# An attention, soft mixture and feed-forward kernel whose attention order is searched at build time and whose copies may change engine

## Chip, cores and metric

The kernel runs on one core of one Trainium2 chip. The metric is the device time of one execution in microseconds (us); for the kernel before, three executions gave 387.11 us as median, from 385.46 to 387.39 us.

## What is computed

Three parts follow each other, cut here to what matters:

```python
# 1 attention, B=4, H=8, S=576, D=64
mask_plain = (rel >= 0) & (rel < 32)                          # heads 0-3
mask_dil = (rel >= 0) & (rel < 128) & (rel % 4 == 0)          # heads 4-7
scores = where(mask, q @ k.T / 8, -1e9)
attn = exp(scores - scores.max(-1)); attn /= attn.sum(-1) + 1e-9
x = (attn @ v).transpose(0, 2, 1, 3).reshape(2304, 512)
# 2 soft mixture of experts, 8 experts with 4 slots each
logits = x @ phi                                              # 2304 x 32
d = softmax(logits, over tokens);  slot_input = d.T @ x
slot_out[e] = relu(slot_input[e] @ w1[e]) @ w2[e]             # w1: 512x1024, w2: 1024x512
y = softmax(logits, over slots) @ slot_out
# 3 feed-forward, d_ff = 2048
h = y @ w_in;  out = (max(h, 0) + alpha * min(h, 0)) @ w_out
```

## The kernel before

The kernel has three stages in one program. **Attention** works on 16 units (a batch and two heads) of nine blocks of 64 queries; eight blocks form a group, so there are 18 groups `g`. A group goes through a fixed chain of steps:

- `sm` and `s` (PE, L273 and L282): the mask is put into a PSUM bank, then 32 matmuls add the scores.
- `max` and `sub` (DVE, L293, L296), `exp` (ACT, L299), `sum` and `rec` (DVE, L303, L307, L308), `norm` (POOL, L312).
- `t` (PE, L317): four transposes; `te` (ACT, through `copy`, L346): two copies of 64x512 from PSUM into `pt_m`.
- `pv` (PE, L330): 32 matmuls; `ev`: their eviction into `xt`, one half on ACT (L346), the other on DVE (L348).

Around these stand the steps of a unit. `qx` (`emit_qx`, L252) spreads a unit's loaded queries into two padded copies, one half of the partitions on ACT (L346) and the other on DVE (L348). When a unit is complete, `lt` (L360) adds its part of the logits; for every second unit `x` and `xe` (L401, L404) transpose tokens and copy them into `xs_m`, on ACT, DVE, ACT in turn; once a batch, `nmax`, `dexp`, `lts`, `lrun`, `dT`, `dTe`, `part` and `acc` (L363 to L421) carry the running softmax over tokens.

All loads are issued by SP, in one order: `q` and `k` of a pair of units (L250, 576 KB each; the first pair in 288 KB pieces), `v` of a unit (L259, 576 KB), and expert weights `w` (L187, 1 MB each; 12 have a buffer of their own, `w0` to `w11`). A `q` load waits until the `qx` copies have emptied the buffer, a `v` load until the `pv` of four units before has read it. A load that waits holds up every load behind it on SP.

The order of the whole stage is written by `schedule` (L82). `tasks_of_attention` (L428) lists tasks with their engine, what they need, a key (a due time, `PERIOD` 4.3 us a group) and two costs from the table `COST`: how long the engine is occupied and after how long the result is there. `schedule` holds a clock for each engine (and one for the DMAs), takes again and again the task that could start first, the smaller key among equals, emits it, and moves that engine's clock on. It adds a margin where a result crosses engines: 0.6 us if PE is the one that waits, 0.25 us for the others here. So it is a plan made at build time; on the chip each engine keeps the planned order and waits on semaphores. The planned order is the only thing that the chip sees of it.

After `schedule` (L548) a hand-written tail (L557 to L600) finishes the last batch. Then the **mixture** stage reads 32 weights of 1 MB (`emit_l1` L622, `emit_l2` L637 to L653), its order written by hand, and the **feed-forward** stage starts with `conv(0, 0)` (L701, ACT), which needs the first feed-forward weight (L185, `w_f`, the 33rd 1 MB load) and stands behind the copy L753 on ACT. The feed-forward stage is planned by the same `schedule`, with costs, places and keys of its own (L937).

## Time and profile before

| | us |
|---|---|
| median of three executions | 387.11 (385.46 to 387.39) |
| the profiled execution | 387.63 |
| its span, first to last instruction | 385.9 |
| PE busy | 366.5 (95%) |
| DVE busy | 261.9 (68%) |
| ACT busy | 217.2 (56%) |
| POOL busy | 144.0 (37%) |
| DMA | 75.19 MB, mean 195 GB/s |

The profiled execution took 1.7 us more than its span, the time outside the first and last instruction. A share of busy time is an average over three stages with different limits: attention with its tail fills the span to about 99 us, the mixture to about 140 us, the feed-forward the rest. The DMA engines work until about 150 us nearly without a break and little after that. Matmuls are pipelined and the profile models their ends, so a PE that is shown as busy may still run at half its clock; the granted clock is shown beside it.

### The profile page before, as it was taken

The page shows a single profiled execution, that of the slowest core. Times are in us where ns is not written, and L with a number is a line of the kernel's source. Part 1 is how long each engine was busy: PE and PEld are TensorE (multiplying, and loading weights), DVE is VectorE, ACT ScalarE, POOL GpSimd, SP SyncE. Part 2 cuts the span into 40 slices and gives each one's busy share as a digit, 9 for nine tenths or more (in the row PEclk, how much of TensorE's full clock was granted, in tenths as well). Part 3 has the DMA queues.
Part 4 walks back from the last instruction along what each step waited for, and adds up shares of the span by engine and source line. Part 5 has one row for each costly group of instructions (what it writes and reads, how often), then busy time and mean ns, then how long its engine had stood idle before and what let it go on. Part 6 is the DMA issues. An engine that isn't in the chain of part 4 may idle for free.

```text
span 385.9 us, 7887 instructions
## 1 busy us (share of the span) xinstructions
PE 366.5 (95%) x3126; PEld 273.7 (71%) x3126; DVE 261.9 (68%) x452; ACT 217.2 (56%) x467; POOL 144.0 (37%) x125
## 2 busy tenths in 40 slices
PE   8599998998999988899999999999999999999995
PEld 4488786765444357577877787877788878878884
DVE  5968977874237439999999998939974324234263
ACT  2657777675123228888766846646654545446460
POOL 4322222230000004555455566445564444444460
PEclk9979999999899998999999999999999999999999
DMA  8989999999999996053233225000000000001336
GB/s 297 415 324 395 413 414 359 404 416 419 420 419 422 417 422 245 10 207 118 102 112 124 104 100 204 15 0 0 3 1 0 2 0 0 3 0 62 103 122 205
DMA packets 15156, 75.19 MB, mean 195 GB/s; under 512 B 1904, under 2 KB 2304, under 8 KB 8976
## 3 DMA queue, kind: packets, MB, share of 16 engines
q1 hardware_dynamic: 14144, 72.98, 48.5%
q10 hardware_dynamic: 912, 1.64, 1.2%
q8 instruction: 24, 0.39, 0.4%
q14 instruction: 12, 0.10, 0.1%
q0 software_dynamic: 64, 0.07, 0.1%
HBM read 69.97 MB, written 4.72 MB: 194 GB/s over the span
## 4 chain that ended last, share of the span: by engine, by line
PE 57%; DVE 24%; DMA 7%; ACT 5%; issue 4%; POOL 1%; SPq 0%; DVEq 0%; ACTq 0%; POOLq 0%
PE y L835 31%; DMA q_m<-qk 6%; DVE gs L829 5%; PE h L629 4%; PE o L651 4%; PE pv L330 3%; PE hb L821 2%; DVE wo_lo L718 2%; PE s L282 2%; DVE e_m L705 2%; DVE pt_m L711 2%; DVE e_m L708 2%; PE si L410 2%; PE x L401 2%; DVE e_m L703 1%
## 5 line engine op out<-in xcount | busy, mean ns | idle before, releaser
L929 POOL TENSOR_TENSOR gls<-gs,ghs 128x384 fp32r<-128x384 f32 x96 | 118.6, 1252 | 166.6 <-ACT ghs L346 138.3
L835 PE MATMUL y<-wo_hi,ghs 128*128 128x512 f32 x289 | 96.6, 398 | 1.0 <-ACT ghs L346 0.7
L829 DVE SCALAR_TENSOR_TENSOR gs<-gs,beta_s,hb 128x384 f32<-128x384 f32 x96 | 56.4, 609 | 50.5 <-ACT gs L923 48.5
L835 PE MATMUL y<-wo_lo,ghs 128*128 128x512 f32 x289 | 88.7, 392 | 0.0
L835 PE MATMUL y<-wo_hi,gls 128*128 128x512 f32 x289 | 85.8, 393 | 2.7 <-POOL gls L929 2.6
L923 ACT ACTIVATE gs<-hb 128x384 f32<-128x384 f32 x96 | 44.7, 492 | 36.3 <-PE hb L821 28.6
L835 PEld LDWEIGHTS y<-wo_hi,gls 128*128 128x128 f32 x289 | 54.0, 188 | 15.2 <-POOL gls L929 4.8
L346 ACT CAST ghs<-gs 128x384 fp32r<-128x384 f32 x96 | 49.4, 517 | 26.6 <-DVE gs L829 26.2
L835 PEld LDWEIGHTS y<-wo_hi,ghs 128*128 128x128 f32 x289 | 53.4, 188 | 14.6 <-issue 1.8
L835 PEld LDWEIGHTS y<-wo_lo,ghs 128*128 128x128 f32 x289 | 54.0, 188 | 10.4 <-issue 0.2
L312 POOL TENSOR_TENSOR e_m<-e_m,l 128x512 f32<-128x512 f32 x18 | 19.7, 1094 | 60.9 <-DVE l L308 48.5
L821 PE MATMUL hb<-cpack,mpack 128*128 128x384 f32 x96 | 31.3, 345 | 0.2
L282 PE MATMUL s<-q_m 128*64 128x64 f32 x576 | 21.7, 232 | 1.8 <-DVE l L307 1.4
L282 PEld LDWEIGHTS s<-q_m 128*64 128x64 f32 x576 | 19.5, 145 | 4.8 <-issue 2.4
L330 PEld LDWEIGHTS pv<-pt_m,v_m 128*64 128x64 f32 x576 | 19.0, 143 | 4.8 <-ACT pt_m L346 2.6
L346 ACT COPY pt_m<-t 64x512 f32<-64x512 f32 x36 | 20.8, 578 | 2.7 <-PE t L317 2.1
L330 PE MATMUL pv<-pt_m,v_m 128*64 128x64 f32 x576 | 21.0, 229 | 0.3
L821 PEld LDWEIGHTS hb<-cpack,mpack 128*128 128x128 f32 x96 | 17.9, 188 | 4.0 <-DVE gs L829 0.9
L348 DVE COPY xt<-pv 128x256 f32<-128x256 f32 (+7 forms) x32 | 9.6, 305 | 11.8 <-ACT xt L346 11.6
L703 DVE TENSOR_SCALAR pt_m<-pt_m 128x1024 f32<-128x1024 f32 (+1 forms) x9 | 8.1, 901 | 13.9 <-ACT pt_m L701 13.9
L632 ACT ACTIVATE v_m<-h,rinv 128x256 f32<-128x256 f32 x8 | 3.8, 474 | 22.2 <-PE h L629 22.2
L346 ACT COPY xt<-pv 128x256 f32<-128x256 f32 (+7 forms) x32 | 8.7, 279 | 10.8 <-DVE xt L348 6.5
(157 smaller groups left out, 501.7 us busy)
## 6 DMA issues: line engine op xcount, KB each, us to landing
w<-w SPq DMA_DIRECT2D x23, 1024.0 KB, 11.7
v_m<-v SPq DMA_DIRECT2D x16, 576.0 KB, 7.7
q_m<-w_f SPq DMA_DIRECT2D x8, 1024.0 KB, 4.9
q_m<-qk SPq DMA_DIRECT2D x13, 576.0 KB, 6.8
v_m<-w_f SPq DMA_DIRECT2D x7, 1024.0 KB, 4.9
q_m<-w SPq DMA_DIRECT2D x4, 1024.0 KB, 16.2
v_m<-w SPq DMA_DIRECT2D x2, 1024.0 KB, 15.0
q_m<-qk SPq DMA_DIRECT2D x4, 288.0 KB, 5.4
```

Of the source, the lines that this page charges most:

```text
L282: mm(s[r:r + 64, col:col + 64], lhsT=q_of(u)[:, 2 * o:2 * o + 64], rhs=keys(u, c, x), start=False, stop=True, skip_group_check=True)
L312: nc.gpsimd.tensor_tensor(out=e, in0=e, in1=bc(e_[g, "l"], 128, 8, 64), op=ALU.mult)
L330: mm(pv[hs, n], lhsT=vv[u % 4][:, c, hs], rhs=pts[:, NBS * (g % 2) + n, h], start=True, stop=True, skip_group_check=True)
L346: nc.scalar.copy(out=out, in_=in_)
L629: mm(h[32 * g:32 * g + 32, 0:256], lhsT=slotT[:, k, :], rhs=w[:, k % 2, 256 * g:256 * g + 256], start=(k == 0), stop=(k == 3), skip_group_ ...
L651: mm(o[32 * g:32 * g + 32, :], lhsT=ht[:, 4 * r + g, 28 - 4 * e:60 - 4 * e], rhs=w[:, g, :], start=(e == 0 and r == 0), stop=(e == NE - 1 ...
L703: nc.vector.tensor_scalar(out=t, in0=t, scalar1=2.0 ** -15, scalar2=FMAX, op0=ALU.max, op1=ALU.min)
L821: mm(hb[i], lhsT=mpack[:, 128 * f:128 * f + 128], rhs=cpack[:, t0:t0 + 384], start=True, stop=True)
L829: nc.vector.scalar_tensor_tensor(out=g, in0=g, scalar=beta_s[:, f:f + 1], in1=hb[i], op0=ALU.mult, op1=ALU.add)
L835: mm(y[steps[s][0], t][:, sl], lhsT=g, rhs=wo_hl[p == 1][:, f, sl], start=start, stop=stop, skip_group_check=True)
L923: lambda s=s, i=i: nc.scalar.activation(out=half(gs, s, i, 4), in_=hb[i], func=AF.Relu, scale=-1.0),
L929: lambda s=s, i=i: nc.gpsimd.tensor_tensor(out=half(gls, s, i, 6), in0=half(gs, s, i, 4), in1=half(ghs, s, i, 6).bitcast(F32), op=ALU.subt ...
```

## The change

`schedule` is split in two. `plan` makes one order, as `schedule` did, from the keys and from a choice of engine for the tasks that may have several. `schedule` calls it once with the old keys and the first choice, and then, for attention, 2500 times more: each round adds random numbers to the keys of 1, 3 or 10% of the tasks (loads excepted) and redraws a third of that share of the engine choices. It goes on from a round whose planned end is not later than the one it came from by more than a small random allowance, and keeps the earliest planned end of all. The planned end leaves the `w` loads out. The seed is fixed. The order kept is then emitted. The feed-forward's call has no rounds, so there `plan` runs once.

```diff
+ROUNDS = 2500
+def plan(tasks, key, pick, succ, place, lag, readers, margin, begin, mode):
...
+    def spec(name):
+        t = tasks[name]
+        return t[4][pick[name]] if name in pick else (t[0], *t[4:6])
...
+            if best is None or (at, key[name]) < best[0]:
+                best = (at, key[name]), name
...
+def schedule(tasks, place=lambda name: None, lag=lambda name, x: 0.0, readers=lambda name: (), margin=0.06, begin={},
+             mode=lambda name: None, rounds=0, spread=(2, 6, 15), counts=lambda name: True):
...
+    def run(key, pick):
+        p = plan(tasks, key, pick, succ, place, lag, readers, margin, begin, mode)
+        return (max(e[0] for n, e in p[1].items() if counts(n)), p) if p else (1e9, None)
+
+    best, p = run(key, pick)
+    top = best, p, pick
+    for _ in range(rounds):
+        k, c, share, width = dict(key), dict(pick), rng.choice((0.01, 0.03, 0.1)), rng.choice(spread)
+        for n in k:
+            if tasks[n][0] != "dma" and rng.random() < share:
+                k[n] += rng.uniform(-width, width)
+            if n in c and rng.random() < share / 3:
+                c[n] = rng.randrange(len(tasks[n][4]))
+        e, q = run(k, c)
+        if e <= best + 0.25 * rng.random() ** 3:
+            best, p, key, pick = e, q, k, c
+            if e < top[0]:
+                top = e, q, c
+    p, pick = top[1:]
+    for n in p[0]:
+        tasks[n][1](*((tasks[n][4][pick[n]][0],) if n in pick else ()))
```

The tasks with a choice, and what else moves: `qx` may go to ACT, DVE or POOL (there as a product with ones), `te`, `ev` and `xe` to ACT or DVE, each with a planned cost by engine. `s` and `pv` are now chained to the group before, `dexp` to the batch before, `xe` to the `qx` of units 2 and 3, whose raw queries lie in the same buffer. The addition of 1e-9 in `rec` becomes a `tensor_tensor` with a tile that a new memset fills.

```diff
+        if eng == "pool":
+            nc.gpsimd.tensor_tensor(out=out, in0=in_, in1=ones_s[r].rearrange("p (a b) -> p a b", b=1).to_broadcast([64, S // 32, 32]),
+                                    op=ALU.mult)
...
-        nc.vector.tensor_scalar(out=l, in0=l, scalar1=1e-9, scalar2=None, op0=ALU.add)
+        nc.vector.tensor_tensor(out=l, in0=l, in1=eps_s.to_broadcast([128, 8]), op=ALU.add)
...
-        copy("act", pts[r, n:n + NBS, :, x], t_[g][r].rearrange("p (n h q) -> p n h q", h=2, q=32))
+        copy(eng, pts[r, n:n + NBS, :, x], t_[g][r].rearrange("p (n h q) -> p n h q", h=2, q=32))
...
-                        eng = ("act", "dve")[h]
-                        task(("qx", u, h), eng, lambda u=u, h=h, e=eng: emit_qx(u, h, e),
-                             [("q", u if p == 0 else 2 * p)] + ([("s", last[u - NQ])] if u >= NQ else []), k - 5.0, "qx%d" % h)
+                        either(("qx", u, h), lambda e, u=u, h=h: emit_qx(u, h, e),
+                               [("q", u if p == 0 else 2 * p)] + ([("s", last[u - NQ])] if u >= NQ else []), k - 5.0,
+                               **dict([("act", 0.67), ("dve", 0.62)][::1 - 2 * h] + [("pool", 1.15)]))
...
-                task(("te", g, x), "act", lambda g=g, x=x: emit_te(g, x), [("t", g), ("pv", g - 2)], k + 6.0)
+                either(("te", g, x), lambda e, g=g, x=x: emit_te(g, x, e), [("t", g), ("pv", g - 2)], k + 6.0, act=0.58, dve=0.67)
...
-                    task(("ev", g, u, x), eng, lambda g=g, u=u, x=x, e=eng: emit_ev(g, u, x, e), [("pv", g)] + old,
-                         k + 9.0 + x)
+                    either(("ev", g, u, x), lambda e, g=g, u=u, x=x: emit_ev(g, u, x, e), [("pv", g)] + old, k + 9.0 + x,
+                           **dict([*cols(w).items()][::1 - 2 * x]))
...
-        schedule(tasks_of_attention(), readers=readers, margin=0.25, begin=BEGIN, mode=lambda name: MODE.get(name[0]))
+        schedule(tasks_of_attention(), readers=readers, margin=0.25, begin=BEGIN, mode=lambda name: MODE.get(name[0]),
+                 rounds=ROUNDS, counts=lambda name: name[0] != "w")
```

## Rows read from the trace of the kernel before

**Rows 1.** Chain of waits that ended last, 133 to 150 us: start, length, what.

```profile
139.02 1.04 PE o L651 x8
140.08 0.04 ACT acc_m L753
140.56 0.68 ACT pt_m L701
```

**Rows 2.** L185's instructions from 120 to 121 us, with issue and time to landing.

```profile
L185 SPq DMA_DIRECT2D q_m<-w_f x1: 327/327/327, 120.1 to 120.1; - x1
DMA to landing us min/median/max: 19.8/19.8/19.8
```

**Rows 3.** Stretches of the span: length, busy time of each engine, granted clock, DMA.

```profile
24.00:27.00 3.00, 3.00 (x57) 2.31 (x53) 1.59 (x4) 1.24 (x4) 1.04 (x1) 0.94 0.54 131
27.00:60.00 33.00, 31.38 (x620) 25.02 (x619) 27.34 (x68) 25.16 (x58) 8.41 (x8) 1.00 1.02 408
60.00:64.00 4.00, 4.00 (x55) 2.26 (x53) 3.87 (x10) 3.20 (x7) 0.28 (x1) 1.00 0.79 277
64.00:83.00 19.00, 18.38 (x370) 14.78 (x370) 15.08 (x40) 13.72 (x34) 5.39 (x5) 1.00 1.01 409
83.00:140.00 57.00, 54.77 (x642) 27.39 (x636) 23.27 (x58) 16.38 (x43) 1.98 (x3) 0.97 1.01 420
```

**Rows 4.** What SP's queue waited for until 90 us: total, times, longest.

```profile
SPq L259 <- PE pv L330: 23.4, 10, 4.8
SPq L250 <- DVE q_m L348: 19.6, 6, 5.8
```

**Rows 5.** Two more stretches, as in rows 3.

```profile
8.00:18.00 10.00, 6.30 (x145) 4.87 (x139) 8.82 (x18) 4.83 (x10) 2.28 (x2) 0.98 1.02 405
18.00:24.00 6.00, 5.72 (x81) 5.01 (x83) 3.61 (x10) 3.14 (x6) 1.24 (x1) 0.50 1.02 415
```

**Rows 6.** Timeline of PE, 15 to 100 us: start, length, instruction, idle time before it.

```profile
18.28 1.12 PE L282 MATMUL s<-q_m 128*64 128x64 f32 x16 [1.44 <-DVE l L307]
...
20.81 1.98 PE L330 MATMUL pv<-pt_m,v_m 128*64 128x64 f32 x32
...
27.39 1.15 PE L330 MATMUL pv<-pt_m,v_m 128*64 128x64 f32 x32
...
59.77 0.63 PE L317 MATMUL t<-eye_s,e_m 128*128 128x128 f32 x4 [1.50 <-DVE xs_m L348]
...
91.68 0.53 PE L360 MATMUL lt<-xt,phi_s 128*32 128x192 f32 x6 [0.93 <-DVE xt L348]
```

**Rows 7.** L250's instructions from 11 to 11.2 us.

```profile
L250 SPq DMA_DIRECT2D q_m<-qk x1: 327/327/327, 11.0 to 11.0; - x1
DMA to landing us min/median/max: 7.1/7.1/7.1
```

**Rows 8.** Timeline of all engines, 0 to 22 us.

```profile
10.08 1.25 ACT L346 COPY q_m<-xs_m 64x576 f32<-64x576 f32 x2 [2.03 <-DMA xs_m<-qk]
...
11.23 0.62 ACT L299 ACTIVATE e_m<-e_m 128x512 f32<-128x512 f32 x1
...
14.26 1.04 POOL L312 TENSOR_TENSOR e_m<-e_m,l 128x512 f32<-128x512 f32 x1 [8.97 <-DVE l L308]
```

**Rows 9.** Groups by line and shape, 0 to 105 us: busy, mean ns, idle before.

```profile
L312 POOL TENSOR_TENSOR e_m<-e_m,l 128x512 f32<-128x512 f32 x18 | 19.7, 1094 | 60.9 <-DVE l L308 48.5 <-PE x L401 4.9 <-ACT xt L346 4.1
...
L348 DVE COPY q_m<-q_m 64x576 f32<-64x576 f32 x14 | 7.4, 529 | 1.5 <-DMA q_m<-qk 1.1
...
L307 DVE TENSOR_SCALAR l<-l 128x8 f32<-128x8 f32 x18 | 2.9, 161 | 0.1
...
L368 DVE TENSOR_TENSOR nrun<-nrun 96x1 f32<-96x1 f32 x3 | 0.5, 156 | 0.1
```

**Rows 10.** Timeline of all engines, 59 to 61 us.

```profile
59.24 1.04 POOL L312 TENSOR_TENSOR e_m<-e_m,l 128x512 f32<-128x512 f32 x1 [2.68 <-DVE l L308]
...
59.66 0.94 DVE L348 COPY q_m<-q_m 64x576 f32<-64x576 f32 x1
```

More of the change, by code (lines that the diff above doesn't have):

```diff
@@ L1 @@
+import random
 from contextlib import ExitStack
@@ L79, in constants, with begun, enter @@
     return np.concatenate([eye] + [mask[:, n % NST].reshape(128, 128) for n in range(NST + 2)], axis=1)
-def schedule(tasks, place=lambda name: None, lag=lambda name, x: 0.0, readers=lambda name: (), margin=0.06, begin={}, mode=lambda name: None):
-    left, end_at, clock, wrote, read, ring, now = dict(tasks), {}, dict(begin), {}, {}, [], None
-    while left:
+def plan(tasks, key, pick, succ, place, lag, readers, margin, begin, mode):
+    need = {n: len(set(t[2])) for n, t in tasks.items()}
+    end_at, clock, wrote, read, ring, now, order, ready = {}, dict(begin), {}, {}, [], None, [], {}
+    def spec(name):
+        t = tasks[name]
+        return t[4][pick[name]] if name in pick else (t[0], *t[4:6])
+    def begun(engine, xs):
+        sure = SURE if engine == "pe" else margin
+        return [end_at[x][0] + sure * (end_at[x][1] != engine) + d for x, d in xs if not engine == end_at[x][1] == "pe"]
+    def enter(name):
+        t = tasks[name]
+        ready[name] = max([t[6]] + begun(spec(name)[0], [(x, lag(name, x)) for x in t[2]]))
+    for name in tasks:
+        if not need[name]:
+            enter(name)
+    while ready:
@@ L89, in schedule @@
         best = None
-        for name, (engine, _, need, key, _, _, rd) in left.items():
-            if any(x not in end_at for x in need):
+        for name, at in ready.items():
+            engine = spec(name)[0]
+            at = max(at, clock.get(engine, 0.0))
+            if best is not None and at > best[0][0]:
                 continue
-            full = ring[-3] if readers(name) and len(ring) > 2 else ()
-            if any(x not in end_at for x in full):
-                continue
-            sure = SURE if engine == "pe" else margin
-            at = max([clock.get(engine, 0.0), rd] + [end_at[x][0] + sure * (end_at[x][1] != engine) + lag(name, x)
-                                                     for x in (*need, *full) if not engine == end_at[x][1] == "pe"])
+            if readers(name) and len(ring) > 2:
+                if any(x not in end_at for x in ring[-3]):
+                    continue
+                at = max([at] + begun(engine, [(x, 0.0) for x in ring[-3]]))
@@ L106, in schedule @@
+        if best is None:
+            return None
         (at, _), name = best
-        engine, fn, _, _, occ, lat, _ = left.pop(name)
-        fn()
+        engine, occ, lat = spec(name)
+        del ready[name]
+        order.append(name)
         if readers(name):
@@ L265, in emit_vc @@
         a, b = 128 * (0, 5)[x] + d * (x == 0), 128 * (5, NC)[x]
-        nc.gpsimd.tensor_tensor(out=w[o:o + 32, a:b], in0=w[r:r + 32, a - d:b - d],
-                                in1=ones_s[r:r + 32].to_broadcast([32, b - a]), op=ALU.mult)
+        if eng == "pool":
+            nc.gpsimd.tensor_tensor(out=w[o:o + 32, a:b], in0=w[r:r + 32, a - d:b - d],
+                                    in1=ones_s[r:r + 32].to_broadcast([32, b - a]), op=ALU.mult)
+        else:
+            copy(eng, w[o:o + 32, a:b], w[r:r + 32, a - d:b - d])
     def emit_sm(g):
@@ L346, in copy @@
             nc.scalar.copy(out=out, in_=in_)
+        elif eng == "dve":
+            nc.vector.tensor_copy(out=out, in_=in_)
         else:
-            {"dve": nc.vector, "pool": nc.gpsimd}[eng].tensor_copy(out=out, in_=in_)
+            nc.gpsimd.tensor_copy(out=out, in_=in_)
     def tokens(b, hp, t0, n):
@@ L489, in tasks_of_attention @@
                     p = hp // 2
-                    for m, eng in enumerate(("act", "dve", "act")):
+                    for m in range(3):
                         before = [("ev", f, w, x) for f in range(g + 1) for w in (u - 1, u) for x in range(2)]
@@ L525, in tile_kernel @@
         nc.vector.memset(ones_s, 1.0)
+        nc.vector.memset(eps_s, 1e-9)
         zero = pt_m[:, 0:512]
```

52 lines of the change are left out of this document (35 added, 17 removed).

## The prediction

> **What bounds the kernel now.** The change moves attention only, so I read backwards from where attention's end could matter. The chain of waits shows the start of the feed-forward stage: the mixture's last matmuls at 139.02 us, the copy L753 at 140.08, then `conv(0, 0)` on ACT at 140.56 [rows 1]. That is the chain through PE. A second condition stands right beside it: `conv(0, 0)` reads the first feed-forward weight, issued at 120.1 us and landed 19.8 us later, at 139.9 [rows 2]. So the DMA stream is only 0.6 us ahead of PE's chain. Whatever attention gains beyond 0.6 us arrives only if the stream gains too.
>
> What could the stream gain? The stretches show it full, at 420 GB/s, from 83 to 140 us [rows 3]. There a landing is fixed by the bytes before it. Before 83 us there are holes: 131 GB/s from 24 to 27 us, 277 from 60 to 64, and 408 and 409 in the long stretches [rows 3]. Against 420 these are 3 x (1 - 131/420) = 2.06, 4 x (1 - 277/420) = 1.36, 33 x 12/420 = 0.94 and 19 x 11/420 = 0.50 us, together 4.9 us. The total of bytes is the same after the change, so the first feed-forward weight can land at most 4.9 us earlier, apart from the ramp at the very start. SP's own waits tell where holes come from: 23.4 us for `pv` to free a `v` buffer, 19.6 us for a `qx` copy to free a `q` buffer [rows 4]. While one load waits there, nothing behind it is issued. These are waits for attention's compute, which is what the change reorders.
>
> What could PE gain? Three things stand in its way. From 8 to 18 us it is busy 6.30 of 10 us [rows 5], so 3.70 us idle. From 18 to 24 us it is busy for 5.72 us at a granted clock of 0.50, the 1.2 GHz level [rows 5]; 32 `pv` matmuls take 1.98 us there and 1.15 us at 27.39 [rows 6]. At full clock that work would take some 2.9 us less. This fall of the clock came right after the thin stretch. Later, two waits stand out: 1.50 us before `t` at 59.77, for a `xe` copy on DVE, and 0.93 us before `lt` at 91.68, for an `ev` copy on DVE [rows 6], together 2.43 us. The sum is 3.70 + 2.9 + 2.43 = 9.0 us as the most PE could win back.
>
> **The change, part by part.** *The search over keys and engines.* It emits no new work; it changes who waits for whom. Its planned clock knows neither the granted clock nor late landings, so I price it by what the trace shows as lost.
>
> (a) 8 to 18 us. ACT does two `qx` copies from 10.08 us, which stand ahead of the first `exp` at 11.23, and the first `norm` starts only at 14.26 [rows 8]. Until `norm`, PE has no `t`. An order with `exp` first, or those copies elsewhere, brings the first `t` and `pv` forward by about one pair of copies, 1.25 us, and by the DVE steps that stand between. But 1.44 us of the idle time lies in the middle of an `s` [rows 6], which ended when the keys issued at 11.0 us landed 7.1 us later [rows 7], whatever releaser the row names; an order on PE cannot make them land. That leaves 3.70 - 1.44 = 2.26 us. I take 1.5, nearest to the 1.25 us of copies plus a little; the ends are a loss of another wait of 1.44 and a gain of 3.70.
>
> (b) The half clock. If PE has its `t` and `pv` in the thin stretch, the fall may not come. I take half of 2.9, 1.4 us; the ends are 0 and 2.9, and a further stretch of that kind, -2.9, since a new order can leave PE idle elsewhere.
>
> (c) The two later waits, both for a copy on an engine that the search may now choose. I take half, 1.2 us; the ends are 0 and 2.43.
>
> PE's side then gains 1.5 + 1.4 + 1.2 = 4.1 us.
>
> (d) The stream. The hole at 24 to 27 us is a `v` load that waits for `pv`, and `pv` would come some 3 us earlier by (a) and (b): I take 1.5 of 2.06. The hole at 60 to 64 us is a load that waits for a `qx`: I take half, 0.7 of 1.36. The thin losses, 0.94 + 0.50, I leave but for 0.1. The stream gains 2.3 us; its ends are 4.9 and a loss, priced below, because the planned end that the search minimises leaves out the `w` loads.
>
> *`qx` on POOL.* No row shows it. The nearest are `norm`, 1094 ns for 512 columns [rows 9], which for 576 gives an estimate of 1.23 us, and DVE's own copy at 529 ns [rows 9]. I take 1.23. It is hidden behind POOL's 60.9 us of idle time [rows 9]; if a `norm` comes due behind it, that group is late by up to 1.23 us. A POOL operation also disturbs DVE: the copy at 59.66 us, beside a `norm` at 59.24, took 0.94 us [rows 10] where the mean is 0.529 [rows 9]. The Trainium skill's GPSIMD Engine Reference, section Key points, speaks against the change here: GpSimd shares its SBUF interfaces with VectorE and contends with DVE instructions in a two-port mode or with two SBUF inputs. By that rule every `qx` on POOL makes DVE's neighbouring copies longer, and the sum would hold such pairs; I hold none, since which `qx` move is open and DVE has slack. The trace agrees with it by the one row at 59.66 us.
>
> *`rec`.* 18 additions, 161 ns each before; a `tensor_tensor` of one column took 156 [rows 9]. Between -0.1 and +0.1 us in all on DVE; 0. *The new memset* and *the new needs*: one small DVE instruction in the start-up, at most about 0.16 us by the same rows, beside the first loads; the new needs repeat the order in which PE and ACT already work: 0. *The feed-forward plan* runs once with the costs it had: 0, and its first instruction moves with 140.56 us. The next feed-forward weights lie behind the first in the same stream and move with it.
>
> **The sum.** The feed-forward starts earlier by the smaller of 4.1 us (PE) and 2.3 + 0.6 = 2.9 us (stream). From the profiled 387.63 us this gives 384.7. That execution is 0.5 us above the median of 387.11, so for the median I say 387.1 - 2.9 = 384.2 us. Its own range: from both ends of the stream's gain, 4.9 + 0.6 = 5.5 us less, 381.6, to the bound of what can be told from no change. That bound, 0.5%, is 1.9 us, so up to 385.1.
>
> **Rivals.**
>
> *The stream does not follow* (no change). PE finishes attention earlier, but the holes only move, since each `q` and `v` load still waits for its buffer and a round is judged without the `w` loads. Then PE stands before the last mixture weights and the gain is the 0.6 us of slack: 386.5 us. For it: 43 us of SP's waits are of this kind [rows 4]. Against: both large holes follow late compute.
>
> *The ports* (no change). By the rule above, copies on POOL delay `norm` and stretch DVE's copies. Eight of the 32 `qx` copies there, each beside one copy of DVE, at 0.94 - 0.53 = 0.41 us each on DVE are 3.3 us; PE would keep 4.1 - 3.3 = 0.8 us of its gain: 386.3 us. Against: POOL idles most of attention, and the plan uses a longer cost for POOL than for the others.
>
> *The stream gets worse* (slower). One mechanism: SP's order. In the new order a `q` or `v` load stands ahead of `w` loads while its buffer is still being read, SP waits, and the queue runs empty as from 24 to 27 us. One more hole of that size and one as from 60 to 64 us are 3.4 us; less the 0.6 of slack the start comes 2.8 us later: 389.9 us. It decides from 0.6 us of added hole, and can be told from no change from 2.5. For it: the plan believes that a load is issued on time, and an order tuned to that has less room for lateness. Against: the engines' gains release buffers earlier.
>
> *It does not do what it says*: the kept order is planned earlier, but what was lost was never in the plan (the clock, late keys). It gives the time of the first rival and is counted there.
>
> **How the numbers follow.** Forecast 0.54; the stream does not follow 0.20; the ports 0.06; the stream gets worse 0.20. So faster by over 0.5% 0.54, within it 0.26, slower 0.20. The range goes from the stream's full gain, 381.6, to the price of the slower rival, 389.9; that leaves out half of that rival and a little below.
>
> **What would show it.** In the changed kernel's stretches the hole near 24 us should be nearly closed and the granted clock from 18 to 24 us above 0.50; the first `norm` should start before 13.5 us; the last `lt` should come about 4 us before 91.68. The first feed-forward weight should land near 137.6 us and `conv(0, 0)` start at 137.7. If the last `lt` is early but that landing is not, the first rival holds; if landings of the `w` loads lie later and SP's waits grew, the slower one. I am wrong altogether if `conv(0, 0)` starts 3 us earlier and the end does not.

## The result, and the profile after

The changed kernel takes 390.31 us (median of 13, 387.89 to 394.71) against 387.11 for the kernel before: a ratio of 1.0089, 95% interval 1.006 to 1.0118. That is slower, by what the third rival gave (389.9), and 0.4 us outside the range. Ratios here leave out executions that lie over 1.5% above the fastest of their kernel, while medians and ranges in us are of all (so 394.71 does not count in 1.0089, and one ratio below rests on two of six executions). The profiled execution of the changed kernel is the fastest of its 13, 387.89 us (span 386.1), so its profile shows the change at its best; what an ordinary execution loses has to be read from the experiments.

The chain of waits of the changed kernel where the feed-forward starts (columns as in [rows 1]: start, length, what):

```profile
119.81 19.93 DMA q_m<-w_f
139.81 0.67 ACT pt_m L779
```

`conv(0, 0)` starts at 139.81 us, 0.75 earlier than in [rows 1], and is now released by the landing of the first feed-forward weight itself. That landing moved by 0.2 us only, from 139.94 to 139.74 (119.81 + 19.93). PE was ready sooner. Its timeline (start, length, what, idle time before it and its releaser):

```profile
17.99 1.04 PE L383 MATMUL t<-eye_s,e_m 128*128 128x128 f32 x4 [2.97 <-POOL e_m L378]
...
88.02 1.50 PE L428 MATMUL lt<-xt,phi_s 128*32 128x192 f32 x24
...
96.52 4.48 PE L707 MATMUL h<-w,slotT 128*32 128x256 f32 x48 [0.20 <-DVE slotT L676]
```

The last matmuls of `lt` end at 89.52 (88.02 + 1.50), where in [rows 6] they ended at 92.21 (91.68 + 0.53), and the first `h` of the mixture starts at 96.52, where before it was 99.14. So PE gained 2.6 us on the way, and the weights were not there to use it. The stretches of the changed kernel (stretch, length, then busy us of PE, PEld, DVE, ACT and POOL with their instructions, granted clock, DMA share, GB/s):

```profile
8.00:18.00 10.00, 5.37 (x110) 3.99 (x106) 8.00 (x16) 6.21 (x11) 4.63 (x4) 1.00 1.02 412
18.00:24.00 6.00, 6.00 (x111) 5.36 (x113) 3.53 (x10) 3.15 (x6) 2.08 (x2) 0.72 0.99 367
24.00:27.00 3.00, 3.00 (x77) 2.48 (x73) 2.49 (x6) 2.67 (x7) 1.15 (x1) 1.00 1.03 424
27.00:60.00 33.00, 31.86 (x623) 25.09 (x617) 26.97 (x65) 20.45 (x49) 11.03 (x10) 1.00 0.95 361
60.00:64.00 4.00, 3.90 (x54) 2.39 (x55) 3.90 (x10) 3.86 (x10) 2.42 (x3) 1.00 1.01 419
64.00:83.00 19.00, 18.79 (x387) 15.65 (x383) 16.11 (x44) 14.28 (x39) 6.71 (x7) 1.00 1.02 417
83.00:140.00 57.00, 54.82 (x612) 27.43 (x606) 23.82 (x58) 12.94 (x36) 0.50 (x1) 0.97 1.01 419
```

Both large holes of [rows 3] are closed: 424 GB/s from 24 to 27 us (131 before), 419 from 60 to 64 (277 before). But from 27 to 60 us the stream fell from 408 to 361 GB/s, which against 420 is 33 x 59/420 = 4.6 us. Before, the holes of the stretches from 24 to 83 us made 4.9 us; now they make 4.8, and another 0.8 us is lost from 18 to 24 us, where the stream fell from 415 to 367. The holes moved, and their sum is no smaller.

SP's waits until 90 us (total us, times, longest) and the engines' waits for loads (same columns, from 15 to 92 us):

```profile
SPq L307 <- DVE q_m L414: 18.9, 4, 6.1
SPq L322 <- PE pv L396: 18.4, 8, 4.9
SPq L307 <- PE s L348: 7.4, 3, 3.6
SPq L307 <- ACT q_m L412: 5.3, 3, 2.6
```

```profile
ACT q_m L412 <- DMA q_m<-qk: 9.1, 3, 4.3
POOL q_m L315 <- DMA q_m<-qk: 7.9, 3, 3.8
DVE q_m L414 <- DMA q_m<-qk: 3.6, 2, 2.2
```

The first two rows are 37.3 us here against 43 in [rows 4], but the next two have grown (7.4 us for `s`, 4.5 before; 5.3 us for `qx` on ACT, 0.2 before), so SP waits for buffers as long as it did. Its total does not tell a full stream from a thin one: the nearly full stream of group 6 has rows of the same size (19.0, 18.7, 7.7 and 4.4 us). What did change is on the engines: three of them stand 20.6 us before `qx` copies whose queries have not landed; in the kernel before this was 5.9 us, on ACT alone.

One loss behind the start of the feed-forward is separate: from `conv(0, 0)` to the end of the span it takes 386.1 - 139.81 = 246.3 us, before 385.9 - 140.56 = 245.3. Its plan is not the same. The tasks `('y', 58)` and `('h', 4, 1)` can start at the same time and have the same key; the old loop took the first in the list of tasks, the new one the first in its table of ready tasks, and from there the two orders differ. By the plan's own figures the new order ends at 241.5 us and the old one at 240.6.

A second thing also makes this stage longer or shorter, whatever its order: in some executions the granted clock falls to the 1.2 GHz level for a few us, some 22 to 32 us after `conv(0, 0)`. Two profiles with the old order of this stage, the kernel before and no_rounds of group 5:

```profile
160.00:170.00 10.00, 8.69 (x43) 6.08 (x42) 9.97 (x12) 8.43 (x18) 6.24 (x4) 1.00 0.30 105
160.00:170.00 10.00, 9.52 (x42) 7.38 (x43) 8.26 (x9) 7.46 (x16) 4.76 (x4) 0.83 0.53 185
```

In the second the clock is 0.51 from 162 to 164 us. From `conv(0, 0)` to the end the two take 245.3 and 246.8 us. The 13 profiles with the old order and no such fall take 245.0 to 246.1 us, the four with it 246.5 to 247.0; with the new order it is 246.3 and 246.5 us without and 247.8 with it. So the new order costs about 1 us, and the fall of the clock somewhat over 1 us in the executions that have it; what brings it on is not shown. In no_rounds PE had been busy for 8.8 of the 10 us before 160, but plan_with_late_landings of group 6 has 8.5 there and no fall.

### The profile page after: what moved, and what is told of

Read it like the earlier page. It is cut to its first block, busy times and chain, and to the rows that moved or that the text cites. A ratio compares the mean times of both kernels' runs of the same rounds, so it can differ in the third digit from the quotient of the medians.

```text
span 386.1 us, 7905 instructions
## 1 busy us (share of the span) xinstructions
PE 366.0 (95%) x3126; PEld 272.8 (71%) x3126; DVE 264.1 (68%) x453; ACT 214.0 (55%) x460; POOL 151.5 (39%) x132
## 4 chain that ended last, share of the span: by engine, by line
PE 61%; DMA 19%; DVE 10%; ACT 4%; POOL 3%; issue 2%; SPq 0%; DVEq 0%; ACTq 0%; POOLq 0%
PE y L913 43%; DMA q_m<-qk 6%; DMA q_m<-w_f 5%; DMA w<-w 4%; PE hb L899 4%; PE pv L396 3%; POOL gls L1007 2%; DMA v_m<-v 2%; PE s L348 2%; PE t L383 2%; DVE gs L907 2%; PE si L478 1%; PE h L707 1%; PE x L469 1%; DMA v_m<-w_f 1%
## 5 line engine op out<-in xcount | busy, mean ns | idle before, releaser
L913 PEld LDWEIGHTS y<-wo_hi,gls 128*128 128x128 f32 x289 | 53.9, 188 | 15.3 <-POOL gls L1007 4.7
L899 PE MATMUL hb<-cpack,mpack 128*128 128x384 f32 x96 | 32.6, 350 | 0.6 <-DVE mpack L893 0.2
L378 POOL TENSOR_TENSOR e_m<-e_m,l 128x512 f32<-128x512 f32 x18 | 18.9, 1053 | 32.1 <-DVE l L374 18.1
L412 ACT COPY pt_m<-t 64x512 f32<-64x512 f32 x32 | 18.4, 579 | 4.5 <-PE t L383 3.9
L781 DVE TENSOR_SCALAR pt_m<-pt_m 128x1024 f32<-128x1024 f32 (+1 forms) x9 | 8.9, 990 | 12.0 <-ACT pt_m L779 12.0
L383 PE MATMUL t<-eye_s,e_m 128*128 128x128 f32 x72 | 11.7, 287 | 3.6 <-POOL e_m L378 3.5
L359 DVE TENSOR_REDUCE m<-s 128x8 f32<-128x512 f32 x18 | 12.1, 677 | 3.9 <-PE s L348 3.8
## 6 DMA issues: line engine op xcount, KB each, us to landing
v_m<-w SPq DMA_DIRECT2D x2, 1024.0 KB, 18.7
```

What stands on the lines that cost most here:

```text
L359: nc.vector.tensor_reduce(out=m, in_=by_key(s_[g]), op=ALU.max, axis=AX.X)
L378: nc.gpsimd.tensor_tensor(out=e, in0=e, in1=bc(e_[g, "l"], 128, 8, 64), op=ALU.mult)
L383: tr(part(t, j, 128), part(es[g % 4], j, 128), eye_s)
L412: nc.scalar.copy(out=out, in_=in_)
L781: nc.vector.tensor_scalar(out=t, in0=t, scalar1=2.0 ** -15, scalar2=FMAX, op0=ALU.max, op1=ALU.min)
L899: mm(hb[i], lhsT=mpack[:, 128 * f:128 * f + 128], rhs=cpack[:, t0:t0 + 384], start=True, stop=True)
```

## The experiments

Each ratio is to the kernel before, with its 95% interval. "Early landings" are the table's costs of the change (a `q`/`k` load planned to land 3.6 us after its start, a `v` load 3.7), "late landings" those with 2.5 us added. The runs were made in five sets, in which the kernel before had medians from 385.75 to 387.22 us, so compare ratios and not us across experiments. Where a GB/s stands alone, it is the mean from 20 to 90 us of the profiled execution; against 420 it gives the holes in those 70 us, as 70 x (1 - GB/s / 420). The kernel before has 390, so 5.0 us, and the change 386, so 5.7 us.

**1. Which stage is slower?** The first run keeps the new attention and gives the feed-forward its old order, by breaking ties as the old loop did; the second has the old attention and the new feed-forward order.

```diff
-            if best is None or (at, key[name]) < best[0]:
-                best = (at, key[name]), name
+            k = (at, key[name], rank[name] if rank else 0)
+            if best is None or k < best[0]:
+                best = k, name
```

> The changed kernel with one edit: equal start and equal key in the feed-forward's plan are decided by the order of the task list again, so that its feed-forward has the order of the kernel before; its attention is that of the changed kernel. Theory A (the loss is made by the feed-forward's order, which the rewritten planner changed by deciding ties differently): the feed-forward takes 245.3 us again from conv(0, 0) to the end, which starts at about 139.8, so the time is 386.4 us, 0.7 under the kernel before, and the spread of the changed kernel (387.9 to 392.9) shrinks to that of the kernel before. Theory B (the new attention order makes the loss, through late loads or the engines' state): it stays at 389 to 391 us.

Measured: 1.0121 [1.0067, 1.0174], 390.62 us.

> The kernel before with one edit: its feed-forward is planned by the changed kernel's planner, which gives the changed kernel's feed-forward order; attention is that of the kernel before. Theory A: slower than the kernel before by the loss of the changed kernel plus the 0.7 us that attention gave there, 390 to 391 us, with conv(0, 0) at 140.5 as before. Theory B: 387.1 us, as the kernel before.

Measured: 1.0027 [0.9992, 1.0061], 387.18 us. So the loss is attention's; the feed-forward's order costs some 0.3% here, not clear of zero, while the first run, which has the old order, is 0.3% slower than the change itself (1.0121 and 1.0089), not clear of zero either.

The profile of the second run also says how far one profile can be trusted. It has the attention order of the kernel before, yet its stream is at 402 GB/s, its first `h` starts at 96.98, the weight lands at 137.60 and `conv(0, 0)` starts at 137.67, 2.9 us earlier than in [rows 1]. Its span, 385.5 us, is hardly shorter, since beside the new order that execution has the fall of the clock described above (247.8 us to the end). So the landing and PE's 2.6 us in the profile of the change lie within what one order shows from one execution to the next; the ratios, over many executions, carry the verdicts.

The profiled execution of the first run (390.66 us, its median 390.62) is an ordinary one and shows the loss that the profile of the change doesn't: 373 GB/s, holes of 7.8 us, and the first feed-forward weight at 142.63, 2.7 us later than before, for 2.8 us more of holes than in the profile before. One of its holes can be followed from end to end. Its stretches:

```profile
54.00:56.00 2.00, 2.00 (x32) 1.23 (x27) 0.87 (x2) 0.00 (x0) 0.00 (x0) 1.00 1.03 392
56.00:58.00 2.00, 1.70 (x28) 1.41 (x29) 1.61 (x2) 1.53 (x3) 1.32 (x1) 1.00 0.85 348
58.00:60.00 2.00, 1.64 (x49) 1.44 (x48) 1.90 (x7) 1.94 (x6) 0.20 (x1) 1.00 0.46 89
...
20.00:90.00 70.00, 65.67 (x1265) 51.66 (x1262) 56.27 (x136) 42.73 (x103) 22.58 (x21) 0.99 0.97 373
```

and its timeline, SP's loads first, then the `qx` copies on the three engines:

```profile
49.89 0.80 SPq L309 DMA_DIRECT2D q_m<-qk  x2
50.75 3.04 SPq L324 DMA_DIRECT2D v_m<-v  x2
58.32 0.33 SPq L309 DMA_DIRECT2D q_m<-qk  x1
58.70 1.24 SPq L246 DMA_DIRECT2D w<-w  x1
...
56.44 0.67 ACT L414 COPY q_m<-q_m 64x576 f32<-64x576 f32 x1 [2.60 <-DMA q_m<-qk]
...
56.39 1.78 DVE L416 COPY q_m<-q_m 64x576 f32<-64x576 f32 x2 [1.52 <-DMA q_m<-qk]
...
56.53 1.32 POOL L317 TENSOR_TENSOR q_m<-q_m,ones_s 64x576 f32<-64x576 f32 x1 [3.93 <-PE x L471]
```

Queries issued at 49.89 us reach the copies at 56.4, some 6 us later; ACT and DVE have been standing before them for 2.60 and 1.52 us, with their other work behind. The copies end at 58.2, the last of them the second one of DVE, which stands behind POOL's (see the last section). Only then is the buffer empty, and SP, which has issued nothing since 53.8 us, starts the next `q` load at 58.32, with a `w` load behind it. By then the queue has run dry: 89 GB/s from 58 to 60. A late landing makes a late copy, a late copy a late load, a late load an empty stream. This is the rival's mechanism, in one place.

**2. Is it the last weight alone that counts?** Two kernels leave one load out: the second half of the last expert's second matrix is taken from its first half, so that the first feed-forward weight is one place earlier.

```diff
+        if i == 4 * NE - 1:
+            wt[kind, a, t] = wt[kind, a, 0]
+            return
```

> The first of these kernels (new attention, old feed-forward order), which leaves out the load of the 32nd mixture weight: the second half of the last expert's second matrix is taken from its first half. It takes 1 MB, 2.5 us at 420 GB/s, out of the stream ahead of the first feed-forward weight. Theory of the stream (attention's gain of 2.6 us on PE is lost because that weight lands only 0.2 us earlier): the weight lands near 137.3 us, conv(0, 0) starts at 137.5 to 137.7 as PE allows, and the time falls by 2.1 us against the first kernel, to 384.3. Rival (the gain is lost in the mixture's PE work or in the feed-forward): conv(0, 0) stays at 139.5 or later and the time stays within 0.5 us of the first kernel.

Measured: 1.0091 [1.0058, 1.0124], 389.05 us: a miss, 0.3% under the first run with intervals that overlap, where 384.3 was expected. In the profiled execution, 389.16 us, the weight does land earlier, at 140.44 (142.63 in the first run), but the first `h` starts only at 99.24 us (96.52 in the profile of the change), and `conv(0, 0)` at 142.03, behind PE's chain. The order is the same as in the change; in that execution PE had gained nothing.

> The kernel before, with the same load left out. Theory of the stream with PE's chain ahead at 140.1 there: the weight lands near 137.5, but conv(0, 0) still starts at 140.5, and the time is that of the kernel before within 0.5 us. Rival (the stream alone sets the start): conv(0, 0) starts 2 us earlier and the time falls by 2 us.

Measured: 0.9981 [0.9942, 1.0019], 384.92 us, no difference: before, PE's chain stands 0.6 us behind the stream. Together the two say that the start of the feed-forward is not held by that weight alone, and that the 2.6 us of PE's gain in the profile of the change is a best case.

**3. Is it where the `w` loads stand in SP's order?** In the new plan the 12 `w` loads stand at other places among the 34 `q`, `k` and `v` loads. Each order was run with the other's places.

```diff
+    if rounds:
+        p = places(p[0], tasks), p[1]      # w after load 12, 15, 19, 21, 24, 24, 28, 30, 32, 33, 34, 34
```

> New attention order with the old feed-forward order; only the places of the twelve w loads among the other loads on SP are those of the kernel before (after the 12th, 15th, 19th, 21st, 24th, 24th, 28th, 30th, 32nd, 33rd, 34th, 34th of the q, k and v loads, where the new order has 12, 14, 21, 21, 24, 29, 30, 30, 32, 34, 34, 34). Theory C (the new order leaves q, k and v loads that wait for buffers with no w load in front of them to fill the time, and the stream runs empty): the holes between 28 and 38 and between 50 and 62 us shrink, the first feed-forward weight lands near 139 us instead of 142.6, and the time is 386 to 387.5 us against 387.1 of the kernel before on the same footing, 3 us under the new order with its own places. Rival D (the engines' new order itself runs late, whatever SP does): it stays about 1.2% over the kernel before.

Measured: 1.0087 [1.0054, 1.012], 389.43 us; 368 GB/s. The old places do not cure the new order: its engines wait 33.7 us for queries (the two rows below and 6.6 us on DVE). The waits of its profiled execution and one line of PE's timeline:

```profile
POOL q_m L333 <- DMA q_m<-qk: 16.0, 5, 6.3
ACT q_m L430 <- DMA q_m<-qk: 11.1, 3, 5.0
```

```profile
59.64 1.03 PE L366 MATMUL s<-q_m 128*64 128x64 f32 x16 [2.70 <-DMA q_m<-qk]
```

> The kernel before with the new order's places of the w loads on SP and nothing else. Theory C: holes where five or seven loads stand in a row, the first feed-forward weight later by 2 to 3 us, the time 0.5 to 0.8% over the kernel before. Rival D: the time of the kernel before within 0.3%.

Measured: 1.0107 [1.0065, 1.0149], 390.13 us; 375 GB/s. The new places alone, on the old order, make the whole loss, where Theory C had put 0.5 to 0.8%: up to seven `q`, `k` and `v` loads now stand in a row with no `w` load between them (at most four before). Its stretches:

```profile
30.00:40.00 10.00, 10.00 (x204) 8.29 (x201) 8.71 (x23) 8.38 (x20) 2.86 (x3) 1.00 0.93 307
...
50.00:60.00 10.00, 9.32 (x199) 7.75 (x197) 8.41 (x21) 8.36 (x20) 2.09 (x2) 1.00 0.85 306
```

ACT and DVE wait only 5.2 us for queries there, as in the kernel before. So waits before copies are not the only way to such holes, and either half of the change is enough: its places on the old order, or its order with the old places. That the SP sequence of both does not suit the rest is my reading; no run shows it apart.

**4. A second queue, and a full one.** If SP's in-order waits were all, `w` loads issued by another engine would fill the holes. First by ACT at the places of the plan, then by ACT behind the `exp` of 12 groups, which needs no wait on SP, for both attention orders.

```diff
-            nc.sync.dma_start(out=w, in_={"a": w1, "b": w2}[kind][a, t])
+            (nc.scalar if i < NW else nc.sync).dma_start(out=w, in_={"a": w1, "b": w2}[kind][a, t])
```

> New attention order with the old feed-forward order; the twelve w loads that have buffers of their own are issued by ACT instead of SP, at the same places in the order, so that no q, k or v load that waits on SP holds one up. Theory C: the holes close, the first feed-forward weight lands near 138 us and the time is 1 to 3 us under the kernel before. Rival D: the landings of q and k get later, as they share the engines with w loads, PE waits for them, and the time stays 1% over the kernel before.

Measured: 1.0088 [1.0059, 1.0117], 389.55 us; 374 GB/s. No cure: ACT waits 10.0 us for queries itself (9.8 us in the first run), and what stands behind waits too.

```diff
+            if x[0] == "exp" and x[1] in (1, 2, 3, 5, 6, 7, 8, 10, 11, 12, 13, 14):
+                out.append(ws[at.index(x[1])])          # and issued by ACT, as above
```

> The kernel before; the twelve w loads are issued by ACT right behind the exp of groups 1, 2, 3, 5, 6, 7, 8, 10, 11, 12, 13, 14, so that a load that waits on SP holds none of them up and one or two are always under way. Theory of the stream: the holes after 20 us fall from 4 to 6 us to under 2, the first feed-forward weight lands at 137 us or before, and the time falls by what PE's chain allows, to 385 to 386.5 us. Rival: q, k and v share the engines with w loads and land later, PE waits for them, and the time is above that of the kernel before.

Measured: 1.0413 [1.0365, 1.0461], 403.37 us, by far the worst. Its DMA issues (KB each, median us to landing) and waits:

```profile
w<-w ACTq DMA_DIRECT2D x12, 1024.0 KB, 9.4
q_m<-qk SPq DMA_DIRECT2D x13, 576.0 KB, 9.4
```

```profile
ACT q_m L356 <- DMA q_m<-qk: 11.2, 3, 6.2
...
PE s L292 <- DMA q_m<-qk: 6.8, 2, 4.0
```

A `q` or `k` load now lands 9.4 us after its issue; in the kernel before the median of the same 13 was 6.8. The `w` loads are issued early, the queries come late, and the stream is emptier than ever: 348 GB/s. That the late queries hold up the compute that frees buffers, and so empty it, is the likely link. The Trainium skill's page "DMA: Bandwidth & Descriptors", section "Issuing engines are not separate DMA queues", says that transfers issued by different engines share the same 16 DMA engines; these landings agree: with `w` on ACT's queue but at the places of the plan the median stayed 6.7 us, and it rose where the `w` loads came earlier.

> The changed kernel's attention order with the old feed-forward order, and the w loads issued by ACT behind the exp of the same groups. Theory of the stream alone: holes under 2 us after 20 us, the time 383.5 to 385.5 us, under the kernel before, as PE's chain is 2.6 us earlier there when landings are in time. Theory D: ACT, POOL and DVE still wait 15 us or more for q and k, and the time stays at 388 to 390 us.

Measured: 1.0366 [1.0276, 1.0455], 405.1 us. The same. "Fill the stream" as a rule falls; it matters which load is ahead.

**5. Is it the search, and is it the seed?** The runs of this group all have the old feed-forward order, so they stand beside the first run, 1.0121.

```diff
-    rng, succ = random.Random(1), {}
+    rng, succ = random.Random(2), {}
```

> The changed kernel with the old feed-forward order and seed 2 in place of 1. Its planned end is 88.6 us against 88.2 of seed 1, and 94.2 of the kernel before; its w loads stand after the 12th, 14th, 19th, 21st, 24th, 24th, 28th, 31st, 32nd, 33rd, 34th, 34th load, almost as in the kernel before. Theory C: not slower than the kernel before, 385 to 387 us. Rival D (an order tuned to the plan runs late on the chip): about 1% slower, as seed 1.

Measured: 1.0037 [1.0007, 1.0067], 387.49 us; 395 GB/s. The same change with another seed is nearly as fast as before, with nearly the same planned end (88.6 us in the plan's own figures, 88.2 for seed 1, 94.2 for the order before).

```diff
-    rng, succ = random.Random(1), {}
+    rng, succ = random.Random(3), {}
```

> The changed kernel with the old feed-forward order and seed 3, landings planned as in the change (early). Planned end 89.8 us. Theory D (planned landings): not faster than the kernel before, 386.5 to 390 us, with more than 10 us of waits of ACT, DVE and POOL for q and k. Theory L (luck of the order): anywhere, as likely under as over 386.

Measured: 0.9946 [0.9913, 0.9979], 384.96 us: faster than before, against the expectation. Its planned end, 89.8, is the latest of the three. Its profiled execution was the slowest of its 12, so why it is fast cannot be read from it.

```diff
-ROUNDS = 2500
+ROUNDS = 0
```

> The changed kernel with the old feed-forward order and no rounds of search: the rest of the change alone (other planned costs for copies, the chained needs, tensor_tensor in rec, the new memset). Its planned end is 95.3 us against 94.2 of the kernel before. If the search makes the loss, the time is within 0.4% of the kernel before; if the planned costs or rec make it, 389 us or more.

Measured: 1.0009 [0.997, 1.0048], 386.81 us; 406 GB/s. The new planner without its search is no slower than the kernel before. The other edits (`rec`, the ready table, the new needs, the planned costs of copies) cost nothing that this can tell (0.5%); the loss is in what the search picks.

```diff
-**dict([("act", 0.67), ("dve", 0.62)][::1 - 2 * h] + [("pool", 1.15)])
+**dict([("act", 0.67), ("dve", 0.62)][::1 - 2 * h])
```

> The changed kernel with the old feed-forward order, seed 1 and early landings, but without POOL as a choice for qx. Planned end 90.2 us. If a late load that holds up POOL, and norm behind it, makes the loss, the time is at or under the kernel before, 385 to 387 us; if late loads hold up ACT and DVE as well, 388 to 390.

Measured: 1.0007 [0.9975, 1.0039], 387.18 us; 390 GB/s. Without POOL among the choices the search also ends in another order (planned end 90.2), so this does not price POOL's copies; it is a fourth draw of the lottery. The four draws do follow their waits for queries on ACT, DVE and POOL, if not strictly: 10.4 us here, 11.4 with seed 3, 15.3 with seed 2 and 18.6 with seed 1 go with 1.0007, 0.9946, 1.0037 and 1.0121.

**6. The plan's landings.** The table lets a `q`/`k` load land 3.6 us after its start. On the chip, with the plan's zero at the start of the span, the first ten of the 34 `q`, `k` and `v` loads land within 1.6 us of their planned time; the last ten land 2.0 to 3.5 us after it in the profile before, 3.0 to 3.5 in that of the change and 3.8 to 6.3 in the first run. So the cost was put 2.5 us up, with the old feed-forward order.

```diff
-qq=(1.45, 3.6), v=(1.5, 3.7)
+qq=(1.45, 6.1), v=(1.5, 6.2)
```

> The changed kernel with the old feed-forward order and one other edit: the search plans with a landing of q, k and v loads 2.5 us later than it did (6.1 us for 3.6, 6.2 for 3.7), which is nearer to what the traces show. Its planned end is 92.6 us. Theory D, in the form that it now has (seed 1's order puts qx copies, s and pv where the plan believes the loads landed; on the chip they land 2 to 6 us later and ACT, POOL and DVE wait with everything behind them: 18 to 21 us of such waits against 6 to 7 in the kernel before): these waits fall under 10 us in all and the time is 384 to 386.5 us, not above the kernel before. Rival E (any order found by search loses about 1%, whatever landings it plans with): 389 to 391 us.

Measured: **0.9926 [0.9896, 0.9956]**, 383.63 us (382.51 to 384.3): faster than both kernels. The chain, the waits and the stretches of its profiled execution:

```profile
116.43 20.41 DMA q_m<-w_f
136.92 0.69 ACT pt_m L781
```

```profile
POOL q_m L317 <- DMA q_m<-qk: 4.4, 1, 4.4
ACT q_m L414 <- DMA q_m<-qk: 0.6, 1, 0.6
```

```profile
20.00:30.00 10.00, 10.00 (x202) 8.48 (x199) 7.89 (x22) 4.62 (x13) 2.57 (x3) 0.90 1.01 404
30.00:40.00 10.00, 10.00 (x219) 8.16 (x218) 8.67 (x21) 7.90 (x17) 4.75 (x5) 1.00 1.01 394
...
50.00:60.00 10.00, 9.85 (x224) 8.53 (x221) 8.91 (x20) 6.61 (x18) 3.33 (x3) 1.00 1.02 416
...
20.00:90.00 70.00, 69.34 (x1313) 54.35 (x1310) 58.76 (x146) 46.43 (x109) 20.62 (x20) 0.99 1.02 411
```

Waits for queries fall from 20.6 us to 5.0. Holes are 1.5 us where the kernel before has 5.0 (3.0 in the second run of group 1), the first feed-forward weight lands at 136.85, 3.1 us earlier than in the profile before, and `conv(0, 0)` starts at 136.92, 3.6 us earlier. The plan's own end, 92.6, is 4.4 us later than that of the change, and the chip is faster.

Two things are not separated here. From the fifth on, the loads now land 1.7 to 3.7 us before their planned time, so the plan is not exact but safe: whether the truer duration (6.1 us, where the median from issue to landing is 7.0) or the slack does it is open. And the search has moved the `w` loads too, to stand after load 12, 12, 15, 19, 23, 25, 28, 28, 31, 33, 34, 34, so that again at most four loads stand in a row without one. Group 3 says that the old places alone are no cure for the order of the change; how much of this cure they are is not shown.

The same cost with the feed-forward's new order, which is the changed kernel with this edit alone:

> The changed kernel as it is, its feed-forward order included, with one edit: landings of q, k and v planned 2.5 us later (seed 1). Attention has the order of the run with late landings and the old feed-forward order, which took 0.9926 of the kernel before. If the feed-forward's other order costs what the profiles show, 1 to 2 us, the ratio is 0.995 to 0.998; if it costs nothing, 0.9926 within 0.002.

Measured: 0.9966 [0.9938, 0.9994], 384.41 us. Still faster than before; the feed-forward's order takes back 0.4%, with intervals that overlap, in line with 0.3% in the second run of group 1 and with 1.0 us in the profiles, though the first run of group 1 points the other way.

The other two seeds with late landings:

> Seed 2 with landings planned 2.5 us later. Planned end 92.8 us. Theory D: faster than seed 2 with early landings by 2 to 4 us, 383 to 385.5 us, waits for q and k under 8 us and holes in the stream after 20 us under 2. Theory L: about 387, as that seed or the mean of the seeds.

Measured: 0.9948 [0.992, 0.9977], 384.03 us; 412 GB/s.

> Seed 3 with landings planned 2.5 us later. Planned end 92.7 us. Theory D: 383 to 385.5 us, 2 to 4 us under seed 3 with early landings. Theory L: no order between the two.

Measured: 0.9956 [0.9927, 0.9985], 384.51 us; 409 GB/s. With early landings the three seeds gave 1.0121, 1.0037 and 0.9946; with late ones 0.9926, 0.9948 and 0.9956. Three seeds are few, but all three are now faster than before and within 0.3% of each other, and the holes are 1.5, 1.3 and 1.8 us. Seed 3 alone gains nothing that can be told, where 2 to 4 us were expected: its two intervals overlap.

And 2.0 us more:

```diff
-qq=(1.45, 6.1), v=(1.5, 6.2)
+qq=(1.45, 8.1), v=(1.5, 8.2)
```

> Seed 1, old feed-forward order, landings planned 4.5 us later than in the change. Planned end 104.7 us. If only the order of what waits for what matters and the plan is now safer still, the time is that with 2.5 us, 383 to 385. If the plan now keeps buffers and issues loads later than needed, holes come back and the time is 386 us or more.

Measured: 1.015 [1.0102, 1.0198], 391.35 us. Planned end 104.7. Its stream is full to 70 us and thins after that, and PE is now what is late:

```profile
80.00:90.00 10.00, 8.49 (x142) 5.84 (x137) 8.78 (x23) 5.92 (x18) 2.09 (x2) 1.00 0.95 378
```

So the value has a best range: too early and engines stand before loads, too late and PE falls behind (its first `h` starts at 103.39).

## Why the prediction was wrong

**The step that failed is (d), the stream's gain of 2.3 us.** What bounds the kernel was read rightly: the start of the feed-forward is set by PE's chain and the stream, 0.6 us apart, and a gain of PE alone is worth only that. The two holes I costed closed, as I said. But I counted holes as if each belonged to one late step and would go with it. They belong to the fit of SP's whole sequence to the compute, and a new sequence brings its own. In the best execution the first feed-forward weight came 0.2 us earlier where I said 2.3, and the holes from 20 to 90 us were 5.7 us for 5.0; in an ordinary one they were 7.8, and the weight came 2.7 us later. I also took it that what the start gains the end gains: in two profiles (old_attention_new_ffn, no_rounds) `conv(0, 0)` started 2.9 and 2.7 us earlier and the span was shorter by 0.4 and 1.2 only, as the clock fell later on (and the first has the new feed-forward order).

**The slower rival held**: its mechanism is seen in one hole, and its price came close, in part by luck. It was written as one hole of 2.06 and one of 1.36 us, less the slack, 2.8 us; the ordinary execution of the new attention has 2.8 us more of holes in all, its weight 2.7 us later and its start 2.15 us later, and the rest of its 3.0 us is lost behind that start. What I wrote for it ("an order tuned to that has less room for lateness") is what the late landings showed by removing it. I gave it 0.20. The prediction also had a row that spoke for it and was used for another purpose: a landing took 7.1 us [rows 7], while the plan's table lets such a load land in 3.6. That comparison alone, made before the run, would have moved the weight to this rival.

**(a), 8 to 18 us: half right.** The first `norm` starts at 13.00 (predicted before 13.5). PE's busy time in the stretch fell all the same, 5.37 us after 6.30 [rows 5], and PE waits 2.97 us for the second `norm`. POOL's timeline shows where:

```profile
13.00 1.04 POOL L378 TENSOR_TENSOR e_m<-e_m,l 128x512 f32<-128x512 f32 x1 [1.87 <-DVE l L374]
15.48 1.45 POOL L315 TENSOR_TENSOR q_m<-q_m,ones_s 64x576 f32<-64x576 f32 x1 [1.44 <-DVE m L359]
16.90 1.04 POOL L378 TENSOR_TENSOR e_m<-e_m,l 128x512 f32<-128x512 f32 x1
```

A `qx` stands before it on POOL. The `norm`'s input was ready at 14.88 (the reciprocal on DVE ends there), so it is 2.0 us late: the copy takes 1.45 us, and before it POOL waits for queries, which land at 15.36. I had priced that case ("that group is late by up to 1.23 us") and then taken 0, and the wait for the landing was in no price.

**(b), the clock: right in direction.** From 18 to 24 us the granted clock is 0.72, after 0.50 in [rows 5]. **(c):** both waits are gone; after 18 us no single wait of PE is longer than 0.7 us until 95 us. **PE's side** gained 2.6 us of the 4.1 in the best execution; the profiles of new_attention_old_ffn and of the one with a load less have their first `h` at 99.29 and 99.24, a gain of nothing. It is the same order each time; when loads are late, PE is too, and the old order alone moves by as much (99.14 and 96.98 in two profiles).

**The small terms.** The groups of the changed kernel (busy us and mean ns, idle us before and its releasers):

```profile
L315 POOL TENSOR_TENSOR q_m<-q_m,ones_s 64x576 f32<-64x576 f32 x6 | 7.5, 1258 | 11.6 <-DMA q_m<-qk 7.9 <-PE lt L428 2.2 <-DVE m L359 1.4
L373 DVE TENSOR_TENSOR l<-l,eps_s 128x8 f32<-128x8 f32 x18 | 2.8, 157 | 0.1
```

`qx` on POOL takes 1258 ns as a mean and 1.14 us where nothing disturbs it, estimated at 1.23 us; `rec` 157 ns for 161, so 0 as said. *The feed-forward plan: 0* was wrong: the rewritten planner broke a tie the other way, worth 0.9 us in its own figures and about 1 us in the profiles; of three comparisons of times two say 0.3 to 0.4% and one the opposite, none clear of zero. **The ports** rival was not separated by a run, but its price can be read: against 0.457 us undisturbed, DVE's `qx` copies beside operations of POOL lost 1.0 us in all in the profile before, 1.2 in that of the change and 2.6 in the first run, so the change added 0.2 to 1.6 us on DVE, not 3.3.

**Left open:** why seed 3 with early landings is fast; what makes the clock fall in the feed-forward of some executions; how much of the cure is the places of the `w` loads; what one `qx` on POOL costs by itself; and whether the landings alone, planned as a function of the bytes ahead of them, would let the search gain more than these 0.7%. That was not tried.

## What to carry to other kernels

When an order is searched against a model, ask first which of the model's figures the chip misses, in which direction, and whether the order feeds back on it: a search can spend the slack that hid the error, so a better planned end (88.2 for 94.2) can be a slower kernel. Compare planned with measured landings before searching, plan with landings no earlier than the measured ones, and judge by several seeds and many executions rather than by one of each. And where a planner is rewritten, compare the orders of the stages that were meant to stay the same; ties count.

## What the runs showed of the hardware

- **The time of a load depends on what was issued before it, by whichever engine.** The same 576 KB loads had a median landing of 6.8 us in the kernel before, 6.7 with the `w` loads on ACT's queue at the places of the plan, and 9.4 when these were issued earlier there, where the time rose by 4.1%; with early `w` loads on SP's own queue (plan_with_very_late_landings) it was 9.0.
- **The spread of the executions belongs to the order.** The changed kernel spans 5.0 us from the lowest to the highest of the executions compared (387.89 to 392.88), and the same kernel with late landings 1.0 us (383.98 to 384.96), where the kernel before, run beside it, spans 5.4 (383.0 to 388.4). I had taken the spread for noise of the chip. What makes it is not shown: the other two seeds with late landings span 3.2 us each.
- **A DVE copy that starts inside an operation of POOL ends 0.32 us after it.** Of the two copies of DVE at 56.39 us in new_attention_old_ffn, the first starts 0.14 us before POOL's copy and takes 0.46 us; the second starts inside it, at 56.77, and takes 1.40, to 0.32 us after POOL's end (shortest, median and longest ns):

```profile
L416 DVE COPY q_m<-q_m x2: 457/930/1403, 56.4 to 56.8; 64x576 f32<-64x576 f32 x2
```

The copy in [rows 10] ends at 60.60, 0.32 us after its `norm`. Over all profiles, 74 of the 76 `qx` copies of DVE that start inside a `norm` or a `qx` of POOL end 0.31 to 0.32 us after it, while those with no operation of POOL beside them take 0.44 to 0.46 us. POOL's copy is stretched in turn, from 1.14 us to 1.32 where DVE's starts 0.14 before it and to 1.45 where both start together, at 15.47 in the changed kernel. So it is not a shared rate: one waits for the other. The Trainium skill's "GPSIMD Engine Reference", section "8. Key points", says that the two share SBUF interfaces and contend in some modes; these copies agree.
